# Attention in front of two expert layers: 1/sum by way of device memory, the product with v stored with a step of four, and scaling one pair later

## The chip, the cores and the metric

The kernel runs on one core of a Trainium2 chip. The metric is the time on the device in microseconds (us), the median of several executions; lower is better. The core has five engines that run side by side, each through its own instructions in order: TensorE (PE; its weight loads are shown as PEld), VectorE (DVE), ScalarE (ACT), GpSimd (POOL) and SyncE (SP), which issues all transfers (DMAs) of this kernel. TensorE writes its results into PSUM, which has eight banks per partition; the other data lies in SBUF. GpSimd doesn't work on PSUM in this kernel.

## The reference

```python
scores = np.matmul(q, k.transpose(0, 1, 3, 2)) / sqrt(64)      # 2 batches, 12 heads, 448 tokens, 64 wide
scores = np.where(causal_mask, -1e9, scores)
attn = np.exp(scores - scores.max(-1, keepdims=True))
attn = attn / (attn.sum(-1, keepdims=True) + 1e-9)
x = np.matmul(attn, v)                          # put together as 896 tokens x 768
h = x @ w_in                                    # 768 x 2048
g = np.where(h >= 1, h, np.where(h <= -1, 0, (h + 1) ** 2 / 4))
x = g @ w_out                                   # 2048 x 768
xn = x / np.sqrt(np.mean(x * x, -1, keepdims=True) + 1e-6) * rms_g
out = (silu(xn @ w_gate) * (xn @ w_val)) @ w_out2
```

q, k and v are float32; the weights are float64 and reach the chip as pairs of 32-bit words, so that each weight block has to be put together and split before TensorE can use it.

## The kernel before, in words

**The attention stage.** Heads are worked on in pairs: g runs from 0 to NG - 1 = 11 (six pairs of each batch), and j = 0, 1 are the two heads of a pair, which take partitions 0 to 63 and 64 to 127. The 448 tokens of a head are NCH = 4 chunks of C = 112. A pair has NU = 3 units u: unit 0 is the last query chunk (448 keys), unit 1 the third and the first (336 and 112 keys), unit 2 the second (224 keys). One turn of the loop at line 736 is one step n = 3 g + u, written out by hand in a fixed order for every engine. In a step, TensorE makes the scores of the next unit (line 273) and transposes the exponentials of the unit before (line 304); VectorE adds the mask and takes the maxima of this unit (line 280); ScalarE takes the exponentials with their sums (line 288); ScalarE, and for some VectorE, copy the transposed blocks of two units before out of PSUM (`evac`, lines 322 and 324). The scores rotate through four banks, the transposed blocks and the spread 1/sum through three (`tring`), and the product with v has one bank of its own (bank 7).

**1/sum.** `factor` (lines 330 and 331, VectorE) turns the sums of pair g - 1 into `rs`, 112 partitions x 2 heads x 4 chunks, in step u = 0 of pair g. In u = 1 `spread` brings these onto the layout of the result, 128 partitions x 448 tokens: 16 matmul instructions against the identity (line 338) and one copy by ScalarE into the buffer `rb` (line 340). In u = 2 `pv` multiplies by v (line 352, 20 matmul instructions). In u = 0 of pair g + 1, `xscale` (line 371, VectorE) reads the product from bank 7, multiplies by `rb` and writes the pair's place, and `xsplit` splits it into a rounded part and a rest for the layers that follow (lines 361 and 362, POOL; for pairs of the second batch subtractions by VectorE at line 358 come first). After the loop the same is written out for the last pairs, with the first matmuls of the first layer (`head_in`, `tail_in`, line 665) between them.

**Weights during attention.** The first six weight pieces (four plain blocks, two pairs of blocks) are prepared in small steps placed by hand in the table `EARLY`: (g, u) names the step of the loop, (i, j) the piece and its step. ScalarE scales (line 169), POOL makes low bits (line 180), VectorE joins the words (lines 186 and 198) and forms sums and differences (line 500), ScalarE rounds (lines 205 and 539), POOL makes the rest (lines 206 and 540). Weights arrive in three stage buffers; the last step of a piece issues the next load by SP (`w_next`, line 145). SP also issues the loads of q, k and v (lines 245, 246, 240), all in program order.

**After attention** the first layer runs as products of three operands per feature block (line 665), with weight preparation between the products; then w_out (line 968), normalisation, gate and value (line 665) and the last product (line 1280).

Of the kernel before, what the change touches and what calls it, by code (L numbers as in the profile page):

```python
# [41 lines left out]
def kernel(  # L42
# [17 lines left out]
    C = 112  # L60
# [17 lines left out]
    const = ctx.enter_context(tc.tile_pool(name="const", bufs=1))  # L78
    small = ctx.enter_context(tc.tile_pool(name="small", bufs=4))
    psum = ctx.enter_context(tc.tile_pool(name="psum", bufs=1, space=bass.MemoryType.PSUM))  # L80

# [35 lines left out]
    NPC = C * (NCH * (NCH + 1) // 2)  # L117
    NTB = 3 * NCH + 1
    Pn = AF.at(PO, 2, NPC)
# [4 lines left out]
    mask = AF.at(XFO + S, S)  # L124
    assert XFO + 2 * S <= STO
    poff = [0, C, 3 * C, 6 * C]
# [21 lines left out]

    def w_next(n):
        for i in range(n + 1, len(items)):  # L150
            if items[i][3] == items[n][3]:
                if i - n <= NST:
                    w_load(i)
                return
# [155 lines left out]
    def evac(n, i, eng):  # L310
        g, u = divmod(n, NU)
        PT = PTs[g % 2]
        t = tbank[n][i]
        if u == 2:
            out = PT[:C, :, 1:5:3, :]
            src = t[:C, :4 * C].rearrange("p (j k d) -> p j k d", j=2, k=2)
        else:
            first = 3 if u == 0 else 2
            out = PT[:C, i, first:first + 10:3, :]
            src = t[:C, :4 * C].rearrange("p (k d) -> p k d", k=4)  # L320
        if eng is nc.scalar:
            nc.scalar.copy(out, src)  # L322
        else:
            eng.tensor_copy(out, src)


    def factor(g):
# [4 lines left out]
        return rs  # L332

    def spread(rs, t=None, out=None):
        t = turn(tring) if t is None else t
        for c in range(NCH):
            for j in range(2):
                nc.tensor.matmul(t[D * j:D * (j + 1), c * C:(c + 1) * C], lhsT=rs[:C, j, c:c + 1].to_broadcast([C, D]),  # L338
                                 rhs=ident[:C, :C], start=True, stop=True, skip_group_check=True)
        nc.scalar.copy(rb if out is None else out, t[:, :S])  # L340
# [3 lines left out]
    def pv(g):  # L344
        i = g % 2
        PT = PTs[i]
        xbank[g] = xb = bank(7)
        parts = [(0, 1, C, 3 * C), (0, 11, 0, C)] + [(kc, 4 * kc, kc * C, (NCH - kc) * C) for kc in range(1, NCH)]
        for n, (kc, blk, o, w) in enumerate(parts):
            for j in range(2):  # L350
                src = PT[:C, j].rearrange("p a d -> p (a d)")[:, blk * C:blk * C + w]
                nc.tensor.matmul(xb[D * j:D * (j + 1), o:o + w], lhsT=vraw[i][:C, j, kc, :], rhs=src,  # L352
                                 start=(n == 0), stop=(n == len(parts) - 1), skip_group_check=True)
# [13 lines left out]

    def xscale(g):
        b, p = divmod(g, NP)
        x = xbank[g][:, :S] if g == NG - 1 else rb if b else X0[p]  # L370
        nc.vector.tensor_tensor(out=x, in0=xbank[g][:, :S], in1=qraw[g % NQ] if g == NG - 1 else rb, op=ALU.mult)

    def xsplit(g):
        b, p = divmod(g, NP)
        k = p % HK
        if b == 0:
            pool_split(B21 if p >= HK else B11, k, X0[p])
        elif p < HK:
            sub(rb, rb, X0[p])
            pool_split(T1, k, rb)  # L380
        else:
            t = qraw[g % NQ]
            sub(t, rb, b32(T1[:, 0, k]))
            sub(t, t, b32(T1[:, 1, k]))
            pool_split(T2, k, t)
            pool_split(B22, k, rb)

# [329 lines left out]
    def tail_in(f):  # L717
# [3 lines left out]

    EARLY = {(0, 2): ((0, 0), (0, 1), (1, 0)), (1, 2): ((0, 2),), (2, 0): ((0, 3),), (2, 2): ((1, 1),),
# [6 lines left out]

    def early(g, u):  # L730
        for i, j in EARLY.get((g, u), ()):
            pre[i][j]()

    scores(0)
    w_cap[0] = NA + 4
    for n in range(NN - 1):
        g, u = divmod(n, NU)
        scores(n + 1)
        side = nc.vector if u == 2 else nc.scalar
        old = n >= 2  # L740
# [13 lines left out]
        if u:  # L754
            exps(n, 1)
        if 0 < g and u == 2:
            pv(g - 1)
            load_v(g + 1)
        if n >= 1:
            transposes(n - 1)  # L760
        if u == 0:
            if g > 1:
                xscale(g - 2)
                xsplit(g - 2)
            if g:
                frs = factor(g - 1)
        elif u == 1 and g:
            spread(frs)
            if 1 < g < NG - 1:
                xmix(g - 2)  # L770
        early(g, u)

    n = NN - 1
    maxima(n, 0)
# [571 lines left out]
```

## Time and profile before

| | |
|---|---|
| median of 3 runs | 583.06 us (582.82 to 584.49) |
| profiled execution, its own time | 583.05 us |
| its span in the trace | 581.3 us |
| around the span | 1.75 us |
| granted TensorE clock | 1.00 of full speed throughout |
| TensorE busy | 97% of the span |
| attention stage | to about 104 us of the span |

Times of single instructions below come from the profiled execution and are counted from the start of its span. "Busy" is the time in which an engine had an instruction in work; overlapping instructions count once. The chain of waits is the work that ended last, followed back from the last instruction.

### The profile page before, as it was taken

The page shows a single profiled execution, that of the slowest core. Times are in us where ns is not written, and L with a number is a line of the kernel's source. Part 1 is how long each engine was busy: PE and PEld are TensorE (multiplying, and loading weights), DVE is VectorE, ACT ScalarE, POOL GpSimd, SP SyncE. Part 2 cuts the span into 40 slices and gives each one's busy share as a digit, 9 for nine tenths or more (in the row PEclk, how much of TensorE's full clock was granted, in tenths as well). Part 3 has the DMA queues.
Part 4 walks back from the last instruction along what each step waited for, and adds up shares of the span by engine and source line. Part 5 has one row for each costly group of instructions (what it writes and reads, how often), then busy time and mean ns, then how long its engine had stood idle before and what let it go on. Part 6 is the DMA issues. An engine that isn't in the chain of part 4 may idle for free.

```text
span 581.3 us, 8682 instructions
## 1 busy us (share of the span) xinstructions
PE 566.8 (97%) x3164; PEld 492.5 (85%) x3164; DVE 386.9 (67%) x666; ACT 350.9 (60%) x701; POOL 325.0 (56%) x256
## 2 busy tenths in 40 slices
PE   6999999989899999999999999999999999999997
PEld 3666666878789989999999998999999999999996
DVE  4877788768778877772667668776665656993110
ACT  4988988566667766665634477665545546544111
POOL 3574625845777677995645606566455455991000
PEclk9999999999999999999999999999999999999999
DMA  8334522124542336771443011345333335632002
GB/s 299 106 121 144 205 64 71 55 91 137 177 140 109 108 108 221 255 244 43 166 159 109 0 56 48 116 145 181 109 109 110 114 104 169 211 109 95 1 0 96
DMA packets 17850, 71.34 MB, mean 123 GB/s; under 512 B 2128, under 2 KB 6736, under 8 KB 17808
## 3 DMA queue, kind: packets, MB, share of 16 engines
q1 hardware_dynamic: 17808, 70.79, 36.2%
q8 instruction: 25, 0.41, 0.3%
q14 instruction: 17, 0.14, 0.1%
HBM read 68.03 MB, written 2.75 MB: 122 GB/s over the span
## 4 chain that ended last, share of the span: by engine, by line
PE 84%; DVE 6%; ACT 3%; POOL 3%; issue 2%; DMA 1%; SPq 1%; DVEq 0%; POOLq 0%; ACTq 0%
PE ps L665 34%; PE ps L968 20%; PE ps L1280 15%; PE ps L273 5%; PE ps L352 4%; PE ps L304 4%; PE ps L338 2%; POOL af L180 1%; DMA af<-in_w_in 1%; DVE af L198 1%; DVE af L358 1%; POOL ar L540 1%; DVE ps L450 1%; DVE af L450 1%; DVE af L691 0%
## 5 line engine op out<-in xcount | busy, mean ns | idle before, releaser
L665 PE MATMUL ps<-ar 128*128 128x448 f32 x1260 | 260.3, 367 | 4.9 <-ACT af L846 2.8
L665 PEld LDWEIGHTS ps<-ar 128*128 128x128 f32 x1260 | 235.1, 188 | 28.5 <-ACT af L846 4.3
L206 POOL TENSOR_TENSOR ar<-af,ar 128x768 fp32r<-128x768 f32 (+1 forms) x56 | 93.1, 1664 | 63.0 <-ACT ar L205 52.1
L968 PE MATMUL ps<-ar 128*128 128x448 f32 x576 | 118.1, 366 | 0.0
L968 PEld LDWEIGHTS ps<-ar 128*128 128x128 f32 x576 | 108.0, 188 | 9.2
L180 POOL TENSOR_SCALAR af<-af 128x768 int32<-128x768 uint8 x76 | 85.7, 1128 | 7.6 <-DMA af<-in_w_out 1.5
L1280 PE MATMUL ps<-ar 128*128 128x448 f32 x432 | 87.9, 365 | 0.0
L1280 PEld LDWEIGHTS ps<-ar 128*128 128x128 f32 x432 | 81.1, 188 | 6.7 <-DVE ar L1227 0.3
L198 DVE SCALAR_TENSOR_TENSOR af<-af 128x768 int32<-128x768 int32 (+1 forms) x66 | 72.1, 1095 | 20.3 <-POOL af L180 11.0
L169 ACT ACTIVATE af<-af 128x768 f32<-128x768 f32 x61 | 54.9, 912 | 10.5 <-DMA af<-in_w_out 10.5
L205 ACT CAST ar<-af 128x768 fp32r<-128x768 f32 (+1 forms) x56 | 41.0, 732 | 30.7 <-DVE af L198 14.7
L288 ACT ACTIVATE af<-ps,nm 112x336 f32<-112x336 f32 (+2 forms) x96 | 47.2, 507 | 9.7 <-DVE nm L280 9.6
L904 DVE TENSOR_TENSOR ar<-af,ar 128x448 fp32r<-128x448 f32 x32 | 37.8, 1191 | 21.9 <-ACT ar L903 21.9
L1227 DVE TENSOR_TENSOR ar<-af,ar 128x448 fp32r<-128x448 f32 x24 | 29.2, 1226 | 32.3 <-ACT ar L1226 32.3
L280 DVE CUSTOM_DVE_ANT_0 ps<-ps,af 112x336 f32<-112x336 f32 (+2 forms) x96 | 41.4, 472 | 8.5 <-PE ps L273 7.4
L485 POOL TENSOR_TENSOR ar<-af,ar 128x768 fp32r<-128x768 f32 x18 | 33.7, 1872 | 21.6 <-ACT ar L481 21.6
L273 PE MATMUL ps<-af 64*112 64x448 f32 (+3 forms) x192 | 37.6, 449 | 5.7 <-DVE af L251 4.4
L1061 POOL TENSOR_TENSOR ar<-af,ar 128x448 fp32r<-128x448 f32 x15 | 18.0, 1214 | 31.3 <-ACT ar L1060 15.0
L273 PEld LDWEIGHTS ps<-af 64*112 64x112 f32 x192 | 17.5, 180 | 16.4 <-DVE af L251 4.4
L304 PE MATMUL ps<-ident,af 112*112 112x112 f32 x240 | 30.4, 266 | 0.0
L304 PEld LDWEIGHTS ps<-ident,af 112*112 112x112 f32 x240 | 22.9, 133 | 6.9 <-issue 3.0
L322 ACT COPY af<-ps 112x448 f32<-112x448 f32 x47 | 24.1, 543 | 7.3 <-PE ps L304 7.0
(110 smaller groups left out, 635.9 us busy)
## 6 DMA issues: line engine op xcount, KB each, us to landing
af<-in_w_out SPq DMA_DIRECT2D x28, 768.0 KB, 4.4
af<-in_w_in SPq DMA_DIRECT2D x20, 768.0 KB, 4.4
af<-in_w_gate SPq DMA_DIRECT2D x16, 768.0 KB, 5.0
af<-in_w_val SPq DMA_DIRECT2D x12, 768.0 KB, 4.2
af<-in_kT SPq DMA_DIRECT2D x12, 224.0 KB, 4.5
af<-in_qT SPq DMA_DIRECT2D x12, 224.0 KB, 5.0
af<-in_v SPq DMA_DIRECT2D x12, 224.0 KB, 2.7
out_T<-af SPq DMA_DIRECT2D x12, 224.0 KB, 1.9
```

The lines of the kernel that those rows point to most:

```text
L169: nc.scalar.activation(c, c, ACTF.Prelu, scale=2.0 ** -112, alpha=-2.0 ** 32)
L180: nc.gpsimd.tensor_scalar(out=words(n, 0, I32), in0=b, scalar1=1.0 / 32, scalar2=-31.0 / 64, op0=ALU.mult, op1=ALU.add)
L198: nc.vector.scalar_tensor_tensor(out=out.bitcast(I32), in0=words(n, 1, I32)[:, c], scalar=3, in1=words(n, 0, I32)[:, c], op0=ALU.logical_s ...
L205: nc.scalar.copy(hi, src)
L206: nc.gpsimd.tensor_tensor(out=lo, in0=src, in1=b32(hi), op=ALU.subtract)
L273: nc.tensor.matmul(bs[j][:C, o:o + (c + 1) * C], lhsT=q[r, c * C:(c + 1) * C], rhs=k[r, :(c + 1) * C], start=True, stop=True, skip_group_c ...
L280: nc.vector.tensor_tensor_reduce(out=t, in0=t, in1=mask[:C, S - (c + 1) * C:], scale=-1.0, scalar=3e38, op0=ALU.add, op1=ALU.min, accum_ou ...
L288: nc.scalar.activation(Pn[:C, j, poff[c]:poff[c] + w], sbank[n][j][:C, o:o + w], ACTF.Exp, bias=nm[:C, j, c:c + 1], scale=-1.0, accum_out= ...
L304: nc.tensor.transpose(bs[j][:C, o:o + C], Pn[:C, j, poff[c] + kc * C:poff[c] + (kc + 1) * C], ident[:C, :C])
L665: nc.tensor.matmul(b[:, :S], lhsT=w(a, k), rhs=x[:, c, k], start=first and k == 0 and i == 0, stop=(k == HK - 1 and i == 2), skip_group_ch ...
L968: nc.tensor.matmul(ybs[dm][:, :S], lhsT=w[:, a, dm * P:(dm + 1) * P], rhs=t[:, c], start=(n == 0 and i == 0), stop=(n == NM - 1 and i == 2))
L1280: nc.tensor.matmul(obs[dm][:, :S], lhsT=w[:, a, dm * P:(dm + 1) * P], rhs=t[:, c], start=(kk == 0 and i == 0), stop=(kk == NF - 1 and i == 2))
```

## The change

- `spread` goes for ten of the twelve pairs. Instead `send` writes `rs` to device memory (a row of 2 x 448 numbers, in pieces of 4 numbers = 16 bytes, one per partition and head), in step u = 0, and `fetch` reads the row back twice, each time onto 64 partitions of `rb`, in step u = 2. Pairs 10 and 11 still use `spread`.
- So that a partition's four numbers lie side by side in that row, token c * 112 + i is now at place 4 i + c. `pv` and `spread` write their matmul results into PSUM with a step of four numbers (`chunks`); `kernel` puts the tokens back in order on the host's copy of the output.
- `pv` of pair g - 1 moves from u = 2 to u = 1 of pair g. In u = 2 ScalarE copies the product from bank 7 into SBUF (`keep`), and `xscale` multiplies there, in place, in u = 1 of the pair after; POOL does it for eight pairs, VectorE for the others.
- The loop now runs `pv` up to pair 10; the lines after the loop are as they were, so `pv(NG - 2)`, pair 10, is also run there.
- Some copies of transposed blocks go from ScalarE to VectorE or back (`MOVED`), the first of the thirteen blocks of `PT` is dropped, weight loads that a step would issue wait until u = 2 of the pair (`w_late`), and `EARLY` has other places.

```diff
-    NTB = 3 * NCH + 1
+    NTB = 3 * NCH
...
+    late = []
+    held = [True]
+
+    def w_late():
+        while late:
+            w_next(late.pop(0), True)
+
-    def w_next(n):
+    def w_next(n, now=False):
+        if held[0] and not now:
+            late.append(n)
+            return
...
+    def send(g, rs):
+        rows[g] = row = dram.tile([2, S], F32, tag="row", name="row")
+        nc.sync.dma_start(out=row.rearrange("j (p c) -> p j c", c=NCH), in_=rs[:C])
+
+    def fetch(g):
+        row = rows.pop(g)
+        for j in range(2):
+            nc.sync.dma_start(out=rb[D * j:D * (j + 1)], in_=row[j].partition_broadcast(D))
+
+    def chunks(t, j, c, n):
+        return t[D * j:D * (j + 1), :S].rearrange("p (i c) -> p c i", c=NCH)[:, c:c + n]
...
-                nc.tensor.matmul(t[D * j:D * (j + 1), c * C:(c + 1) * C], lhsT=rs[:C, j, c:c + 1].to_broadcast([C, D]),
-                                 rhs=ident[:C, :C], start=True, stop=True, skip_group_check=True)
+                nc.tensor.matmul(chunks(t, j, c, 1), lhsT=rs[:C, j, c:c + 1].to_broadcast([C, D]),
+                                 rhs=ident[:C, :C].rearrange("k (n i) -> k n i", n=1), start=True, stop=True,
+                                 skip_group_check=True)
...
-        parts = [(0, 1, C, 3 * C), (0, 11, 0, C)] + [(kc, 4 * kc, kc * C, (NCH - kc) * C) for kc in range(1, NCH)]
+        parts = [(0, 0, 1, 3), (0, 10, 0, 1)] + [(kc, 4 * kc - 1, kc, NCH - kc) for kc in range(1, NCH)]
...
-                nc.tensor.matmul(xb[D * j:D * (j + 1), o:o + w], lhsT=vraw[i][:C, j, kc, :], rhs=src,
+                nc.tensor.matmul(chunks(xb, j, o, w), lhsT=vraw[i][:C, j, kc, :], rhs=PT[:C, j, blk:blk + w],
...
-    def xscale(g):
-        b, p = divmod(g, NP)
-        x = xbank[g][:, :S] if g == NG - 1 else rb if b else X0[p]
-        nc.vector.tensor_tensor(out=x, in0=xbank[g][:, :S], in1=qraw[g % NQ] if g == NG - 1 else rb, op=ALU.mult)
+    def home(g):
+        if g < NP:
+            return X0[g]
+        if g < NG - 4:
+            return xbuf
+        return kraw[g - NG + 4] if g < NG - 2 else rb if g < NG - 1 else xbank[g][:, :S]
+
+    def keep(g):
+        nc.scalar.copy(home(g), xbank[g][:, :S])
+
+    def xscale(g, eng=nc.vector):
+        eng.tensor_tensor(out=home(g), in0=home(g) if g < NG - 2 else xbank[g][:, :S],
+                          in1=qraw[g % NQ] if g == NG - 1 else rb, op=ALU.mult)
...
-    EARLY = {(0, 2): ((0, 0), (0, 1), (1, 0)), (1, 2): ((0, 2),), (2, 0): ((0, 3),), (2, 2): ((1, 1),),
-             (3, 2): ((1, 2), (2, 0)), (4, 0): ((1, 3),), (4, 2): ((2, 1),), (5, 2): ((2, 2), (3, 0)),
-             (6, 0): ((2, 3),), (6, 2): ((3, 2), (4, 0)), (7, 0): ((3, 3),), (7, 2): ((4, 1), (4, 2)),
-             (8, 2): ((4, 3),), (9, 0): ((4, 4),), (9, 2): ((4, 5), (4, 6), (5, 0)), (10, 0): ((4, 7),),
-             (10, 2): ((4, 8),), (11, 0): ((4, 9),), (11, 1): ((4, 10),), (12, 0): ((5, 1), (5, 2)),
-             (12, 1): ((5, 3),), (12, 2): ((5, 4), (5, 5), (5, 6), (5, 7)), (12, 3): ((5, 8),),
-             (12, 4): ((5, 9), (5, 10))}
+    EARLY = {(0, 2): ((0, 0),), (1, 2): ((1, 0), (0, 1), (0, 2)), (2, 0): ((0, 3),), (2, 2): ((1, 1),),
+             (3, 2): ((1, 2),), (4, 0): ((2, 0), (1, 3)), (4, 2): ((2, 1),), (5, 2): ((2, 2), (3, 0)),
+             (6, 0): ((2, 3),), (6, 2): ((3, 2), (4, 0), (3, 3)), (7, 2): ((4, 1), (4, 2)), (9, 0): ((4, 3),),
+             (9, 2): ((5, 0),), (10, 0): ((4, 4), (4, 5)), (10, 1): ((4, 6), (4, 7), (4, 8), (4, 9)),
+             (11, 1): ((4, 10),), (12, 0): ((5, 1), (5, 2), (5, 3), (5, 4), (5, 5), (5, 6), (5, 7)),
+             (12, 3): ((5, 8),), (12, 4): ((5, 9), (5, 10))}
...
+    MOVED = [(g, 2) for g in range(NG) if g not in (3,)] + [(g, 0) for g in (0, 2, 3, 4, 6, 7)]
+    SCALED = (0, 1, 2, 3, 4, 5, 7, 8)
...
-        side = nc.vector if u == 2 else nc.scalar
+        side = nc.vector if (g, u) in MOVED else nc.scalar
...
-        if 0 < g and u == 2:
+        if u == 2 and 0 < g < NG - 1:
+            keep(g - 1)
+            fetch(g - 1)
+        if u == 2:
+            w_late()
+        if n >= 1:
+            transposes(n - 1)
+        if u == 0 and g:
+            frs = factor(g - 1)
+            if g < NG - 1:
+                send(g - 1, frs)
+        if u == 1 and g:
             pv(g - 1)
             load_v(g + 1)
-        if n >= 1:
-            transposes(n - 1)
-        if u == 0:
             if g > 1:
-                xscale(g - 2)
+                xscale(g - 2, nc.gpsimd if g - 2 in SCALED else nc.vector)
                 xsplit(g - 2)
-            if g:
-                frs = factor(g - 1)
-        elif u == 1 and g:
-            spread(frs)
-            if 1 < g < NG - 1:
-                xmix(g - 2)
+            if g == NG - 1:
+                spread(frs)
         early(g, u)
 
+    w_late()
+    held[0] = False
...
-    return np.ascontiguousarray(r.results[0]["out_T"].T)
+    out = r.results[0]["out_T"].T.reshape(B, C, S // C, DM)
+    return np.ascontiguousarray(out.transpose(0, 2, 1, 3).reshape(B * S, DM))
```

## Rows read from the trace of the kernel before

**Rows 1.** The page: span, and busy time of two engines over it.

```profile
span 581.3 us, 8682 instructions
PE 566.8 (97%) x3164; PEld 492.5 (85%) x3164; DVE 386.9 (67%) x666; ACT 350.9 (60%) x701; POOL 325.0 (56%) x256
```

**Rows 2.** Busy by window of one pair: window, length, PE, PEld, DVE, ACT, POOL, clock.

```profile
39.90:47.76 7.86, 7.86 (x74) 5.21 (x74) 5.95 (x23) 6.37 (x21) 5.24 (x5) 1.00 0.53 188
47.76:55.61 7.85, 7.85 (x74) 5.20 (x74) 5.94 (x23) 7.70 (x23) 3.15 (x5) 1.00 0.32 90
63.46:71.31 7.85, 7.85 (x74) 5.20 (x74) 6.36 (x23) 7.10 (x23) 5.20 (x5) 1.00 0.56 190
...
79.27:87.60 8.33, 8.33 (x75) 5.37 (x74) 7.19 (x26) 6.98 (x22) 3.31 (x5) 1.00 0.11 29
87.60:95.86 8.26, 8.26 (x74) 5.30 (x73) 6.14 (x21) 7.77 (x23) 2.93 (x2) 1.00 0.09 30
```

**Rows 3.** Chain of waits, one pair: start us, us, what.

```profile
47.76 0.56 PE ps L273 x4
...
49.23 0.92 PE ps L338 x16
...
51.18 2.04 PE ps L352 x20
...
55.61 0.57 PE ps L273 x4
```

**Rows 4.** Chain of waits, the start of the kernel.

```profile
12.43 1.30 DVE af L186
13.72 0.54 DVE ps L280
```

**Rows 5.** Product with v, groups by form: count, busy us, mean ns.

```profile
L352 PE MATMUL ps<-af 112*64 112x336 f32 x80 | 15.2, 459 | 0.0
...
L352 PE MATMUL ps<-af 112*64 112x112 f32 x80 | 7.2, 259 | 0.0
```

**Rows 6.** Chain of waits, the gate and value stage.

```profile
354.07 135.79 PE ps L665 x668
```

**Rows 7.** DMA issues: count, KB each, median us from issue to landing.

```profile
af<-in_v SPq DMA_DIRECT2D x12, 224.0 KB, 2.7
out_T<-af SPq DMA_DIRECT2D x12, 224.0 KB, 1.9
gvec<-in_rms_g SPq DMA_DIRECT2D x1, 3.0 KB, 5.0
```

**Rows 8.** Groups by line to 170 us: copies, products and splits of 448 columns.

```profile
L362 POOL TENSOR_TENSOR ar<-af,ar 128x448 fp32r<-128x448 f32 x15 | 18.5, 1235 | 1.3
...
L324 DVE COPY af<-ps 112x448 f32<-112x448 f32 x13 | 8.0, 616 | 0.0
...
L371 DVE TENSOR_TENSOR af<-ps,af 128x448 f32<-128x448 f32 x11 | 6.9, 624 | 10.9 <-ACT af L288 6.6 <-PE ps L352 4.3
L340 ACT COPY af<-ps 128x448 f32<-128x448 f32 x12 | 6.5, 538 | 2.0 <-PE ps L338 0.7 <-POOL ar L362 0.6
```

**Rows 9.** Waits to 170 us: engine, line, released by; us in total, times, longest.

```profile
POOL ar L361 <- DVE rs L330: 32.9, 10, 5.6
```

**Rows 10.** Timeline after attention: start, us, engine and line, idle before and releaser.

```profile
103.63 0.99 PE L338 MATMUL ps<-ident,rs 112*64 112x112 f32 x16 [0.25 <-DVE rs L331]
...
122.36 1.62 ACT L539 CAST ar<-af 128x768 fp32r<-128x768 f32 x2 [0.68 <-DVE af L500]
...
123.28 3.67 POOL L540 TENSOR_TENSOR ar<-af,ar 128x768 fp32r<-128x768 f32 x2 [9.04 <-ACT ar L539]
...
124.91 2.12 PE L665 MATMUL ps<-ar 128*128 128x448 f32 x9 [1.21 <-ACT af L840]
```

**Rows 11.** Timeline at the start: TensorE's scores around the wait.

```profile
9.98 1.65 PE L273 MATMUL ps<-af 64*112 64x448 f32 x4
...
15.14 1.24 PE L273 MATMUL ps<-af 64*112 64x224 f32 x4 [1.13 <-ACT af L288]
```

More of the change, by code (lines that the diff above doesn't have):

```diff
@@ L79 @@
     small = ctx.enter_context(tc.tile_pool(name="small", bufs=4))
+    dram = ctx.enter_context(tc.tile_pool(name="dram", bufs=2, space=bass.MemoryType.DRAM))
     psum = ctx.enter_context(tc.tile_pool(name="psum", bufs=1, space=bass.MemoryType.PSUM))
@@ L124 @@
     mask = AF.at(XFO + S, S)
-    assert XFO + 2 * S <= STO
+    xbuf = AF.at(XFO + 2 * S, S)
+    assert XFO + 3 * S <= STO
     poff = [0, C, 3 * C, 6 * C]
@@ L314, in evac @@
         if u == 2:
-            out = PT[:C, :, 1:5:3, :]
+            out = PT[:C, :, 0:4:3, :]
             src = t[:C, :4 * C].rearrange("p (j k d) -> p j k d", j=2, k=2)
         else:
-            first = 3 if u == 0 else 2
+            first = 2 if u == 0 else 1
             out = PT[:C, i, first:first + 10:3, :]
@@ L332, in factor @@
         return rs
+    rows = {}
+    def send(g, rs):
[7 more added lines that the diff above has]
+        return t[D * j:D * (j + 1), :S].rearrange("p (i c) -> p c i", c=NCH)[:, c:c + n]
     def spread(rs, t=None, out=None):
@@ L347, in pv @@
         xbank[g] = xb = bank(7)
-        parts = [(0, 1, C, 3 * C), (0, 11, 0, C)] + [(kc, 4 * kc, kc * C, (NCH - kc) * C) for kc in range(1, NCH)]
+        parts = [(0, 0, 1, 3), (0, 10, 0, 1)] + [(kc, 4 * kc - 1, kc, NCH - kc) for kc in range(1, NCH)]
         for n, (kc, blk, o, w) in enumerate(parts):
             for j in range(2):
-                src = PT[:C, j].rearrange("p a d -> p (a d)")[:, blk * C:blk * C + w]
-                nc.tensor.matmul(xb[D * j:D * (j + 1), o:o + w], lhsT=vraw[i][:C, j, kc, :], rhs=src,
+                nc.tensor.matmul(chunks(xb, j, o, w), lhsT=vraw[i][:C, j, kc, :], rhs=PT[:C, j, blk:blk + w],
                                  start=(n == 0), stop=(n == len(parts) - 1), skip_group_check=True)
@@ L375, in xsplit @@
         k = p % HK
+        x = home(g)
         if b == 0:
@@ L378, in xsplit @@
         elif p < HK:
-            sub(rb, rb, X0[p])
-            pool_split(T1, k, rb)
+            sub(x, x, X0[p])
+            pool_split(T1, k, x)
         else:
             t = qraw[g % NQ]
-            sub(t, rb, b32(T1[:, 0, k]))
+            sub(t, x, b32(T1[:, 0, k]))
             sub(t, t, b32(T1[:, 1, k]))
             pool_split(T2, k, t)
-            pool_split(B22, k, rb)
+            pool_split(B22, k, x)
     def xmix(g):
```

## The prediction, made before the changed kernel had run

> **What bounds the kernel now.** I first read the page's engine shares [rows 1]: TensorE is busy for 97% of the span, all other engines for 56% to 67%. That is an average over stages, so next came the chain of waits, which says where TensorE's time sets the end. In the attention stage the chain is TensorE alone for some 70 us: one pair is scores, transposes, spread, product with v, one behind the other, from 47.76 to 55.61, hence 7.85 us a pair, of which the spread takes 0.92 and the product 2.04 [rows 3]. Third, the busy times cut into windows of one pair [rows 2]: PE is full (7.85 of 7.85), ScalarE takes 6.37 us where a pair has no weight step, 7.10 with one and 7.70 with two, VectorE 5.95 to 6.36, POOL at most 5.24. So whatever TensorE no longer does is time won, until ScalarE at 6.4 to 7.7 us becomes the next bound; that margin is the question. Two pairs late in the stage take 8.33 and 8.26 us [rows 2], about 0.9 us over 7.85 together: there VectorE works on 1/sum, scaling, subtraction and weight sums ahead of the maxima of unit 1. Two other places are not bound by TensorE: the start, where the chain runs through VectorE's weight step at 12.43 (line 186, it waits for the first weight load), behind which its maxima start only at 13.72 [rows 4], and the weight chain right after attention, where TensorE stood idle for 1.21 us at 124.91 [rows 10].
>
> **The sum is made** against the profiled execution's 583.05 us (span 581.3 and 1.75 around it); the median of the runs is 583.06, the same for my purpose. A difference below 0.3%, 1.75 us, I take as no change.
>
> **Part 1, ten spreads less on TensorE.** Ten pairs by 0.92 us [rows 3]: -9.2 us, if nothing else becomes the bound. The pair would take 6.93 us.
>
> **Part 2, the product stored with a step of four.** No row of before shows a strided TensorE write. From below: it costs nothing. The two forms of the product differ by 224 columns and by 459 - 259 = 200 ns, so 0.89 ns a column [rows 5]; in the gate and value stage a matmul of 448 columns takes 135.79 / 668 = 0.203 us, 0.45 ns a column [rows 6]. So PSUM takes columns, side by side ones, twice as fast as the product delivers them. From above: a stored number costs twice its present time; 13 products (12, and the doubled one) by 2.04 are +26.5 us, and the two remaining spreads +1.8. I take nothing, because the product runs at half the rate that rows 6 show PSUM to take. The Trainium skill speaks against it: its page "PSUM — Partial Sum Buffer", section "Specifications (TRN2)", gives lines of 8 bytes and says that any access pattern that isn't contiguous slows matmuls significantly. By that rule the sum would land with the second rival below; no row here can confirm or refute it.
>
> **Part 3, ScalarE.** `keep` takes the place of the spread's copy, both one copy of 448 columns, 0.54 us [rows 8]: 0. Net four copies of transposed blocks go to VectorE. A pair without a weight step needs 6.37 us or less, under 6.93. One weight step adds 0.73 (7.10 - 6.37), and most such pairs lose a copy of 0.54, so they stay under 6.93. Pair 6 now holds three such steps: 6.37 + 3 x 0.73 - 0.54 = 8.0, pair 10 two: 7.8, pairs 5 and 9 one without a moved copy: 7.1. The excess over 6.93 adds up to 2.3 us. From below it is 0 where ScalarE's lead takes it up. I take the middle, +1.2. Against that stands the 0.9 us of the two long pairs of before: scaling and subtraction now come behind the maxima of unit 1, so I take that as won. Net +0.3, bounds -0.9 and +1.4.
>
> **Part 4, VectorE and POOL.** Eight scalings (0.62 us each) leave VectorE, four copies (0.62) come: -2.5 us on an engine that isn't the bound. POOL gets eight scalings; the nearest row is its own subtraction of 448 columns, 1.24 us [rows 8], and POOL waited 32.9 us in the stage for VectorE alone [rows 9], so 9.9 us fit: 0. If POOL were late, its splits would be late first, then the scaled q; the latter is made over a pair ahead.
>
> **Part 5, the way through device memory.** Issued by SP: 10 writes and 20 reads of 1/sum, 0.3 to 0.4 us each; SP has nothing else urgent. `send` goes out when `factor` is done, close to the start of u = 1. Behind it in SP's order come the loads of q and k, of v (which waits for the product, some 3.5 us into the u = 1 step), then `fetch`, which waits for the row and for `rb`, and only behind it the late weight loads. Landing: between 1.9 us (a store of 224 KB to device memory) and 5.0 (128 small pieces behind other loads) for the write, 2.7 to 5.0 for the read [rows 7]. So the row is there 2 to 5 us after the send, `fetch` goes out 4 to 5.5 us into the pair, and `rb` is full at 7 to 10.5; POOL wants it at about 7.5, one pair on (6.93 and scale_q's turn). At worst POOL waits 3 us a pair, which it has (5.24 us of work with the heaviest steps, and 1.24 of scaling, against 6.93 leave little there, more elsewhere). I take 0. The cover is POOL's idle time; without it, pair 6 and pair 9, which VectorE scales, and the subtractions from pair 6 on would hold up VectorE and with it the maxima: up to 3 us for each of five, +15 at the far end.
>
> **Part 6, the doubled product of pair 10.** It runs once in the loop and again behind it, in a stretch where TensorE before had no gap but 0.25 us [rows 10]: +2.0 (bounds 0 and 2.04). VectorE's scaling and subtractions of pair 9 come later too, into the same stretch, so TensorE might have waited there without the second product as well.
>
> **Part 7, weight steps.** At the start, the step that waits for the first weight load goes to the next pair; the maxima at 13.72 could start when their scores are done at 11.63, and TensorE's wait behind them, 1.13 us before 15.14, goes, with some 0.4 of follow-up that I estimate: -1.5 (bounds 0 and -2.1, the 13.72 - 11.63) [rows 4, 11]. After attention, the joins and sums of the sixth piece come ahead of other work, so that ScalarE does not wait 0.68 us for them before 122.36, and POOL behind it (idle until 123.28), and the chain through POOL, VectorE and TensorE moves by as much [rows 10]: -0.8 (bounds 0 and -1.2). The held loads are issued at most one pair later, to stage buffers whose data is wanted a pair or more after that: 0.
>
> **The sum:** -9.2 + 0 + 0.3 + 0 + 0 + 2.0 - 1.5 - 0.8 = -9.2, hence 573.9; I say 574.0.
>
> **Rivals.**
> - *ScalarE, or a late 1/sum, becomes the bound in most pairs.* For it: 7.10 us with one step against 6.93, and ScalarE waits in turn for VectorE and TensorE. Against: pairs without a step have 0.5 us to spare. If a pair takes 7.3 us on average in place of 6.93, ten cost 3.7 us, and the full excess of part 3 is in it: about 578, with a reach from 577 to 582. Chance 0.16.
> - *The stored step slows the product (the other side).* Place: line 352, and 338 for two pairs. At twice the time, 574 + 26.5 + 1.8 = 602 us. It turns the result to slower at a lengthening of the product by a third: 9 us over 13 x 2.04. For it: every stored number lies alone, which no row of before shows; against: rows 5 and 6. Chance 0.15. The Trainium skill's page "PSUM — Partial Sum Buffer" (section "Specifications (TRN2)") is on this rival's side; rows so far don't bear it out.
> - *1/sum arrives late and holds up VectorE.* At the far end of part 5, +15: 589; from about 2 us for each of five pairs it undoes the gain. For it: 224 pieces of 16 bytes, smaller than any in rows 7 (24 bytes). Against: some 7 us between send and use. Chance 0.05.
> - *The gain is given back after attention:* the weight chain there is bound by VectorE, ScalarE and POOL and starts from the same loads. If the stage ends 7 us earlier but the weights don't, 581.3 to 584. Against: those loads wait for buffers that the same steps set free, earlier by as much. Chance 0.04.
>
> **Chances and range.** My forecast, 571.5 to 577 by itself, has 0.60. Faster by over 0.3% (below 581.3): the forecast and nearly all of the first rival, 0.75. Within 0.3%: the last rival and the edges of others, 0.06. Slower: the strided product and the late 1/sum, 0.19. For eight in ten the range reaches from 571.5 over the first rival to 583; it leaves out the slow cases (0.19).
>
> **What would show it.** Right: one pair takes about 6.9 to 7.0 us on the chain, line 352 stays at 2.04 us for its 20 instructions and 459 ns in its long form, line 338 appears 32 times, the scores at 15.14 come at about 14, and the wait of 1.21 us after attention shrinks. Wrong: a longer line 352 (strided store); TensorE waits on line 288 or 322 in most pairs (ScalarE); long waits on line 371 or 361 for a DMA into `rb` (late 1/sum); a longer gap after 104 us less the gain (weights).

## The result, and the profile after

The changed kernel takes 575.05 us (median of 4 runs, 573.98 to 575.91), the kernel before on the same chip 583.77 us (median, 582.82 to 585.26): a ratio of 0.9847, with a 95% interval of 0.9818 to 0.9877. The profiled execution took 574.96 us, with a span of 572.9. The page of the changed kernel answers to [rows 1]:

```profile
span 572.9 us, 8453 instructions
PE 558.0 (97%) x3024; PEld 485.4 (85%) x3024; DVE 385.1 (67%) x662; ACT 347.4 (61%) x697; POOL 333.7 (58%) x264
```

TensorE is 8.8 us less busy and the span is 8.4 us shorter; the share of 97% tells nothing. One undisturbed pair on TensorE's timeline of the changed kernel (start, us, line, count; to be set beside [rows 3]):

```profile
34.47 0.64 PE L285 MATMUL ps<-af 64*112 64x224 f32 x4
35.04 0.98 PE L316 MATMUL ps<-ident,af 112*112 112x112 f32 x8
36.05 2.11 PE L378 MATMUL ps<-af 112*64 112x336 f32 x20
38.09 1.01 PE L285 MATMUL ps<-af 64*112 64x448 f32 x4
...
41.41 0.45 PE L285 MATMUL ps<-af 64*112 64x224 f32 x2
```

The spread is gone, and the product with v (now line 378) stands behind the last transposes of the pair (line 316) and ahead of the scores of 448 columns, where the spread was. From 34.47 to 41.41 that is 6.94 us; most undisturbed pairs take 6.84. The windows of one pair of the changed kernel, columns as in [rows 2] (the last two are the DMA engines' busy share and GB/s):

```profile
27.63:34.47 6.84, 6.84 (x57) 4.33 (x57) 6.35 (x22) 5.97 (x22) 5.19 (x7) 1.00 0.84 240
...
48.26:55.41 7.15, 6.92 (x57) 4.34 (x56) 6.20 (x24) 7.15 (x22) 6.04 (x6) 1.00 0.64 143
55.41:62.86 7.45, 7.45 (x56) 4.60 (x56) 5.87 (x18) 7.25 (x24) 6.95 (x7) 1.00 0.77 238
62.86:69.70 6.84, 6.84 (x57) 4.33 (x56) 6.34 (x23) 6.24 (x22) 3.20 (x4) 1.00 0.81 244
69.70:78.15 8.45, 7.13 (x57) 4.33 (x56) 6.01 (x23) 6.16 (x21) 5.04 (x6) 1.00 0.27 78
78.15:86.73 8.58, 7.65 (x56) 4.58 (x56) 8.10 (x24) 8.22 (x26) 5.81 (x5) 1.00 0.22 58
```

The reader sees four kinds of pair. Where nothing disturbs it, PE fills the window (6.84 of 6.84). In the windows from 48.26 and 55.41 ScalarE fills the first (7.15 of 7.15) and nearly the second (7.25 of 7.45). In the second PE shows as full too, 0.61 us above its 6.84: a wait between the matmuls of one group counts as busy. In the one from 69.70 no engine fills the window, so something is waited for; in the last, VectorE and ScalarE are both over 8.

The wait from 69.70 on is followed through four engines in the timeline of the changed kernel (in brackets the idle time before, and who ended it):

```profile
72.67 1.13 POOL L405 TENSOR_TENSOR af<-af 128x448 f32<-128x448 f32 x1 [1.80 <-ACT af L300]
...
73.84 0.63 DVE L384 TENSOR_TENSOR af<-af 128x448 f32<-128x448 f32 x1 [2.34 <-POOL af L405]
...
74.86 0.45 ACT L300 ACTIVATE af<-ps,nm 112x224 f32<-112x224 f32 x1 [2.29 <-DVE nm L292]
...
75.88 0.31 PE L316 MATMUL ps<-ident,af 112*112 112x112 f32 x1 [1.12 <-ACT af L334]
```

POOL scales pair 7 late (line 405); VectorE's subtraction waits for it (384), the maxima behind that hold up ScalarE's exponentials (300), and the copy behind them holds up TensorE (316). The scaling reads no result of the line that its row names as releaser; what it needs besides the kept product, written by 68.3, is 1/sum (the run with the later weight load, below, names it).

**Where the time went**, from the same points of the two profiled executions:

| stretch (start of the named work, before, after) | before | after | difference |
|---|---|---|---|
| to the scores at 24.12, 20.79 | 24.12 | 20.79 | -3.33 |
| nine pairs, to the scores at 95.86, 86.73 | 71.74 | 65.94 | -5.80 |
| to the last spread, at 103.63 [rows 10], 96.19 | 7.77 | 9.46 | +1.69 |
| to the product of the first layer at 172.86, 165.15 | 69.23 | 68.96 | -0.27 |
| to the end of the span | 408.4 | 407.7 | -0.7 |

The last line belongs to layers that the change doesn't touch. Nine pairs at 6.84 in place of 7.85 would be -9.1, and -5.80 came: the changed kernel has 3.3 us more of stalls in them than the kernel before.

### The profile page after: what moved, and what is told of

Same layout as the page of the kernel before. It is cut to its first block, busy times and chain, and to the rows that moved or that the text cites. A ratio compares the mean times of both kernels' runs of the same rounds, so it can differ in the third digit from the quotient of the medians.

```text
span 572.9 us, 8453 instructions
## 1 busy us (share of the span) xinstructions
PE 558.0 (97%) x3024; PEld 485.4 (85%) x3024; DVE 385.1 (67%) x662; ACT 347.4 (61%) x697; POOL 333.7 (58%) x264
## 4 chain that ended last, share of the span: by engine, by line
PE 71%; ACT 3%; DVE 2%; POOL 2%; issue 1%; POOLq 0%; DVEq 0%
PE ps L701 35%; PE ps L1011 20%; PE ps L1323 15%; POOL af L192 1%; ACT af L181 1%; DVE af L210 1%; DVE ps L486 0%; DVE af L486 0%; POOL af L724 0%; POOL ar L507 0%; PE ps L1096 0%; DVE ps L210 0%; DVE af L727 0%; ACT af L883 0%; ACT ar L516 0%
## 5 line engine op out<-in xcount | busy, mean ns | idle before, releaser
L192 POOL TENSOR_SCALAR af<-af 128x768 int32<-128x768 uint8 x76 | 83.9, 1104 | 7.7 <-DMA af<-in_w_out 1.5
L285 PE MATMUL ps<-af 64*112 64x448 f32 (+3 forms) x192 | 35.8, 452 | 5.0 <-DVE af L263 4.4
L1269 ACT CAST ar<-af 128x448 fp32r<-128x448 f32 x24 | 13.3, 566 | 23.7 <-PE ps L1323 23.7
```

Source lines behind the costliest of these rows:

```text
L192: nc.gpsimd.tensor_scalar(out=words(n, 0, I32), in0=b, scalar1=1.0 / 32, scalar2=-31.0 / 64, op0=ALU.mult, op1=ALU.add)
L285: nc.tensor.matmul(bs[j][:C, o:o + (c + 1) * C], lhsT=q[r, c * C:(c + 1) * C], rhs=k[r, :(c + 1) * C], start=True, stop=True, skip_group_c ...
```

## The experiments

The runs of one kernel spread over 1 to 8 us, so the worth of a single place is read from these points of the profiled executions, and the medians say whether the whole moved.

### Does a step of four cost anything?

**The product stored side by side** (1/sum keeps the order of its row, so numbers meet the factor of another token, and the output has other values):

```diff
-        return t[...].rearrange("p (i c) -> p c i", c=NCH)[:, c:c + n]
+        return t[...].rearrange("p (c i) -> p c i", c=NCH)[:, c:c + n]
```

> The changed kernel with one edit: the product with v and the two remaining spreads are stored side by side again instead of with a step of four (1/sum stays in the order of the row, so numbers meet the factor of another token). Theory (the step is free, because this product writes a column only every 0.89 ns): within 1 us of the changed kernel, 574 to 576 us, line 378 with 458 ns in its long form as now. Rival (the step costs something that the other savings hide): faster than the changed kernel by 2 us or more, and the long form below 450 ns.

Measured: 577.35 us (573.52 to 578.78), ratio 0.9866 [0.983, 0.9901]; last spread at 96.18, as in the changed kernel (96.19). The median lies 1.4 us above the range that was expected; the six runs spread over 5 us, and at the last spread the two kernels stand equal. By form, with the step (changed kernel) and then side by side (count, busy us, mean ns):

```profile
L378 PE MATMUL ps<-af 112*64 112x336 f32 x104 | 19.7, 458 | 0.0
...
L378 PE MATMUL ps<-af 112*64 112x112 f32 x104 | 9.4, 259 | 0.0
```

```profile
L378 PE MATMUL ps<-af 112*64 112x336 f32 x104 | 19.7, 458 | 0.1
```

The mean is that of [rows 5] to a nanosecond, with the step and without. So the step is free here. That doesn't say why, which the next two runs ask.

**The same step where columns come twice as fast.** In both runs the matmuls of line 701 (the first layer, and gate and value) use only the upper halves of weights and activations, as bf16; the second also stores them with the step, so the layers see reordered columns (lines shortened):

```diff
-    nc.tensor.matmul(b[:, :S], lhsT=w(a, k), rhs=x[:, c, k], ...
+    nc.tensor.matmul(b[:, :S], lhsT=w(a, k).bitcast(BF16)..., rhs=x[:, c, k].bitcast(BF16)..., ...   # first run
+    nc.tensor.matmul(b[:, :S].rearrange("p (i c) -> p c i", c=NCH), ...            # second run
```

> The changed kernel, in which the matmuls of the first layer (448 columns each, line 701) take only the upper 16 bits of weights and activations, as bf16, and store side by side: the partner for the next run. Its values are then coarser; the number of instructions stays. Both theories: a matmul of 448 columns there takes 0.19 to 0.21 us, as in the gate and value stage of the kernel before (0.203 us).

> As the run before, but each matmul of the first layer stores its 448 columns with a step of four, as the product with v does. Theory A (a step is free only because the product delivers a column per 0.89 ns, half of what PSUM takes): here, at about 0.45 ns a column, each matmul gets longer, towards 0.4 us, and the stage nearly doubles. Theory B (a step of four costs nothing at any rate): the same mean time as in the run before within 2%.

Measured, one run each: 568.89 us and 783.9 us. By form, side by side and then with the step:

```profile
L701 PE MATMUL ps<-ar 128*128 128x448 bf16 x1260 | 252.0, 358 | 6.4 <-ACT af L891 2.7 <-DVE af L729 1.8 <-POOL ar L507 0.6
```

```profile
L701 PE MATMUL ps<-ar 128*128 128x448 bf16 x1260 | 474.6, 577 | 0.0
```

Matmuls overlap, so the busy time over the count is the rate: 252.0 / 1260 = 0.200 us for 448 columns, 0.45 ns a column; with the step 474.6 / 1260 = 0.377 us, 0.84 ns a column. The 222.6 us more account for the 215.2 us by which the span grew (566.8 to 782.0). So theory B is out and theory A's forecast came: a stepped store of bf16 matmuls goes in at about 0.84 ns a column. The fp32 product delivers one per (458 - 259) / 224 = 0.89 ns by its mean times, whose ends are modelled; by its starts in the changed kernel (336 columns at 23.08, the next 336 at 23.36, the next matmul at 23.64) it is 0.28 us for 336, 0.83 ns a column. So the product is no faster than the step allows, but there is no margin either that these runs could show. That the rate is the reason, and not the type of the operands, is argued: the two runs change the rate by the type. The Trainium skill's page "PSUM — Partial Sum Buffer", section "Specifications (TRN2)", holds that any access pattern that isn't contiguous slows matmuls significantly. The bf16 run agrees with it (0.45 to 0.84 ns a column), the product with v doesn't (459 and 458 ns).

### What opened the pair?

The prediction credited the pair's gain to the ten spreads alone. Four runs separate them from the other thing that moved on TensorE, the product (from the step of unit 2 to that of unit 1).

**Kernel before, ten spreads' matmuls left out** (ScalarE's copy kept, on 112 partitions; 1/sum does not reach those ten pairs):

```diff
-        for c in range(NCH):
+        for c in range(NCH if mm else 0):
...
-        nc.scalar.copy(rb if out is None else out, t[:, :S])
+        nc.scalar.copy((rb if out is None else out)[r], t[r, :S])
...
-            spread(frs)
+            spread(frs, mm=g == NG - 1)
```

> The kernel before with one edit: the matmuls of ten of the twelve spreads are left out, the copy by ScalarE stays (1/sum does not reach those ten pairs). Theory (the stage is bound by TensorE and ten spreads are worth 0.92 us each): 583.5 - 9.2 = about 574 us, with pairs of 6.9 us on TensorE. Rival (without the other rearrangements ScalarE and VectorE become the bound at once): 577 us or more, with waits of TensorE on lines 288 and 322.

Measured: 585.11 us (581.84 to 589.5, 12 runs), ratio 1.0017 [0.9991, 1.0042]: nothing gained. In seven of the twelve the mean granted clock of TensorE is 0.993 or 0.994; in the profiled one it is 0.50, the lower of the two levels, from 20 to 24 us of the span, behind 4 us (14 to 18) in which TensorE was busy for 2.3. The other five, at 0.999 or 1.000, have a median of 582.59 us, 0.8 below the kernel before on the same chip (583.39), where 9.2 were expected. The chain of waits, one pair at full clock (start, us, what):

```profile
36.65 1.80 PE ps L273 x4
38.45 2.04 PE ps L353 x20
40.49 0.91 PE ps L304 x8
41.40 0.95 PE ps L273 x8
42.35 0.53 PE ps L304 x4
...
44.49 1.82 PE ps L273 x4
46.30 2.04 PE ps L353 x20
```

A pair is still 7.85 us, from 38.45 to 46.30. The scores of 448 columns now take 1.8 us where they had 1.04: they absorb what the spread gave up. The timeline of the same run says for what they wait (PEld is TensorE's weight load):

```profile
42.91 0.53 ACT L322 COPY af<-ps 112x448 f32<-112x448 f32 x1
43.42 0.54 ACT L288 ACTIVATE af<-ps,nm 112x336 f32<-112x336 f32 x1
...
45.04 0.21 ACT L288 ACTIVATION_READ_ACCUMULATOR af<-ps,nm 112x1 f32 x1
...
45.30 0.27 PEld L273 LDWEIGHTS ps<-af 64*112 64x112 f32 x2 [0.57 <-ACT af L288]
```

That is a closed loop over two engines. On TensorE: product 2.04, transposes 0.91, scores 0.95, transposes 0.53 (to 42.88); then on ScalarE the copy of those transposes from 42.91 and, behind it in its order, the exponentials up to 45.25 (45.04 + 0.21); these free the bank in which the second half of the next scores goes (45.30), and behind them stands the next product (46.30). The trace of the kernel before has the same loop:

```profile
26.35 0.21 ACT L288 ACTIVATION_READ_ACCUMULATOR af<-ps,nm 112x1 f32 x1
26.51 0.37 PEld L273 LDWEIGHTS ps<-af 64*112 64x112 f32 x4
26.52 1.10 PE L273 MATMUL ps<-af 64*112 64x448 f32 x4
```

The four loads take 0.37 us, not 0.27 as in the changed kernel (at 24.31): those of the second half begin at 26.61, 0.05 us behind the end of the exponentials (26.56), as in the run without spreads (45.30 and 45.25), and the scores take 1.03 us up to the product at 27.55, where the changed kernel takes 0.94 (38.09 to 39.03 above). So the loop was the longer one even then, by some 0.1 us against TensorE's own sum of 7.76 (the changed kernel's 6.84 and the spread's 0.92). The chain showed no wait, because it lay between the matmuls of one group.

**Changed kernel, product put back to the step of unit 2:**

```diff
         if u == 2 and 0 < g < NG - 1:
+            pv(g - 1)
+            load_v(g + 1)
             keep(g - 1)
...
         if u == 1 and g:
-            pv(g - 1)
-            load_v(g + 1)
```

> The changed kernel with one part undone: the product with v (and the load of the next v) goes back from u = 1 to u = 2, ahead of the copy that empties its bank; 1/sum still goes through device memory. Theory (before, a loop took 7.85 us a pair beside TensorE's own sum: product, transposes, scores and transposes on TensorE, then a copy and the exponentials of unit 1 on ScalarE, which the next scores wait for; the earlier place of the product is what breaks it): pairs of 7.7 to 8.0 us and 581 to 585 us, although ten spreads are gone. Rival (the spreads alone are the gain, as the prediction has it): pairs of 6.85 us and about 573 us, the second product of pair 10 being gone too.

Measured: 587.9 us (586.28 to 591.07), ratio 1.009 [1.0066, 1.0114], with pairs of 7.85 us (products at 25.59 and 33.45) and longer, so above the 581 to 585 that were expected. The clock is not the reason: the one run with a mean of 1.000 took 586.73. With every other part of the change in place, and ten spreads gone, the whole gain is gone.

**Kernel before, product early, spreads kept** (and the second product not made):

```diff
-        if 0 < g and u == 2:
+        if n >= 1:
+            transposes(n - 1)
+        if 0 < g and u == 1:
             pv(g - 1)
             load_v(g + 1)
-        if n >= 1:
-            transposes(n - 1)
...
-    pv(NG - 2)
```

> The kernel before with one part of the change: the product of pair g - 1 (and the load of the next v) moves from u = 2 to u = 1, ahead of the spread, and pair 10's product behind the loop is left out since the loop now makes it. All spreads stay. Theory: TensorE's own sum stays 7.85 us a pair, so 582 to 584 us, no change. Rival (the place of the product is the whole gain): 576 us or less.

Measured: 588.86 us (588.03 to 589.35), ratio 1.0098 [1.0085, 1.0112]: slower, which neither theory had. TensorE's timeline of this run, behind product and spread:

```profile
36.53 1.01 PE L273 MATMUL ps<-af 64*112 64x448 f32 x4
38.15 0.98 PE L304 MATMUL ps<-ident,af 112*112 112x112 f32 x8 [0.61 <-ACT af L322]
```

The spread now comes behind the product, ScalarE's copy of it later still, and the copy of the transposed blocks, in order behind that one, holds up the transposes: pairs of 8.29 us (33.72 to 42.00).

**Both edits on the kernel before** (no row sent through device memory, no work moved between engines; 1/sum does not reach ten pairs): the two diffs on the kernel before together.

> The kernel before with both: the product in u = 1 and the matmuls of ten spreads left out, their copies kept (1/sum does not reach those pairs); no transfers, no work moved between engines. Theory (both together, neither alone, open the pair): 6.9 to 7.1 us a pair, 573 to 577 us. Rival (copies and scalings on other engines have to move as well): 579 us or more, with waits of TensorE on ScalarE in most pairs.

Measured: 576.24 us (575.65 to 577.11), ratio 0.9885 [0.9871, 0.9898], pairs of 6.84 to 7.6 us. So, as ratios to the kernel before: spreads out 1.0017, product early 1.0098, both 0.9885: each alone gains nothing, and together they open the pair.

### The smaller terms

**The second product of pair 10 left out** (nothing else of the computation changes):

```diff
     xmix(NG - 3)
-    pv(NG - 2)
```

> The changed kernel with one edit: the second product of pair 10, behind the loop, is left out. Theory of the prediction (TensorE has no gap there): faster by up to 2.0 us, about 573. Rival (VectorE's scaling and subtractions, which also moved there, are the next wait): within 0.7 us of the changed kernel, with a new wait of TensorE for line 342 or 343.

Measured: 573.62 us (572.13 to 577.64), ratio 0.9826 [0.9794, 0.9857]. From one remaining spread to the other it takes 4.22 us (89.76 to 93.98) in place of 5.94 (90.25 to 96.19): the second product costs 1.7 us.

**The first weight steps as before the change:**

```diff
-    EARLY = {(0, 2): ((0, 0),), (1, 2): ((1, 0), (0, 1), (0, 2)), ...
+    EARLY = {(0, 2): ((0, 0), (0, 1), (1, 0)), (1, 2): ((0, 2),), ...
```

> The changed kernel with one edit: the weight steps of the first two pieces at the start are placed as before, so VectorE's sign step comes ahead of the maxima of pair 1. Theory: slower by 1.5 to 2.3 us than the changed kernel, with the scores now at 13.95 us at about 15.1. Rival (the margin at the start is used up by another wait): within 0.7 us.

Measured: 577.14 us (575.76 to 579.69), ratio 0.9881 [0.9853, 0.9908]. The first scores after the wait come at 15.79 (changed 13.95), those one pair on at 23.25 (changed 20.79), and the 2.5 us stay to the last spread (98.69 and 96.19). Part of it is a later landing: POOL, for which VectorE's step waits, begins on the first weight load at 12.18 in this run, in the kernel before at 11.49:

```profile
12.18 0.87 POOL L179 TENSOR_SCALAR af<-af 128x768 f32<-128x768 f32 x1 [2.58 <-DMA af<-in_w_in]
```

```profile
11.49 0.90 POOL L167 TENSOR_SCALAR af<-af 128x768 f32<-128x768 f32 x1 [2.54 <-DMA af<-in_w_in]
```

So by this run the start is worth between 1.8 and 2.5 us. The kernel before against the changed one gives 2.3: the 3.33 us of the table less the 1.01 that this pair gains like every other.

**The weight load held in pair 7, issued one pair later:**

```diff
-        if u == 2:
+        if u == 2 and g != 7:
             w_late()
```

> The changed kernel with one edit: the weight load held in pair 7 is issued in pair 8 instead. In the changed kernel pair 9 takes 8.4 us, VectorE waits 2.34 us for POOL's scaling, which starts late after the reads of 1/sum. Theory (that weight load, 768 KB, delays q and 1/sum on the way): VectorE's wait goes below 1 us, pair 9 below 7.6, and 0.8 to 1.5 us are won, some of which pair 10 may give back. Rival (the scaling is late for another reason): same wait, within 0.7 us.

Measured: 575.67 us (573.82 to 576.23), ratio 0.9868 [0.9852, 0.9885]; last spread at 94.37, pair 9 takes 7.16 us (69.66 to 76.81) and VectorE's wait in it 1.04. POOL's scaling of pair 7, first in the run with the plain store, whose order of instructions here is the changed kernel's, then in this one:

```profile
72.62 1.14 POOL L405 TENSOR_TENSOR af<-af 128x448 f32<-128x448 f32 x1 [1.84 <-DMA af<-row]
```

```profile
71.30 1.14 POOL L405 TENSOR_TENSOR af<-af 128x448 f32<-128x448 f32 x1 [1.14 <-DMA af<-row]
```

Both rows name the read of 1/sum: the scaling starts when that has landed. SP's rows show one reason why it is late: it issues the two reads, which wait until the row is written, from 66.94 with the load later, right behind the load of v (66.44), but from 67.89 in the changed kernel and 68.81 in the run with the plain store. How much the load does is less plain: in six executions whose order of instructions is the same up to there, the two pairs around it (from 62.86 to 78.15 in the changed kernel) take 14.4 us twice and 14.8 to 15.4 four times, with the load later 14.0 and 14.1 (the second is the last run below). So 1/sum comes late by chance of the landing too, and moving the load takes between 0.3 and 1.3 us off these two pairs; the median doesn't show it.

**The sixth weight piece's steps as before the change:**

```diff
-             (11, 1): ((4, 10),), (12, 0): ((5, 1), (5, 2), (5, 3), (5, 4), (5, 5), (5, 6), (5, 7)),
-             (12, 3): ((5, 8),), (12, 4): ((5, 9), (5, 10))}
+             (11, 1): ((4, 10),), (12, 0): ((5, 1), (5, 2)), (12, 1): ((5, 3),),
+             (12, 2): ((5, 4), (5, 5), (5, 6), (5, 7)), (12, 3): ((5, 8),), (12, 4): ((5, 9), (5, 10))}
```

> The changed kernel with the steps of the sixth weight piece after attention back where they stood before the change (two in the first place, one in the second, four in the third). Theory A (the prediction's part 7): the new places gain 0.8 us, so this run is 0.8 us slower than the changed kernel, span about 573.7. Theory B (bringing them forward puts VectorE's sums ahead of the clips that TensorE waits for, and loses what it gains): span 572.2 to 572.9, and the wait of TensorE on the clip, 1.64 us in the changed kernel, falls back towards 1.2 us or less.

Measured: 576.68 us (574.16 to 579.01), ratio 0.9881 [0.9854, 0.9907], which doesn't tell it from the changed kernel. TensorE after attention, changed kernel and then this one:

```profile
96.19 0.99 PE L364 MATMUL ps<-ident,rs 112*64 112x112 f32 x16
...
115.46 4.83 PE L701 MATMUL ps<-ar 128*128 128x448 f32 x21 [1.64 <-DVE af L727]
...
165.15 15.06 PE L701 MATMUL ps<-ar 128*128 128x448 f32 x73 [0.36 <-POOL ar L507]
```

```profile
94.88 0.99 PE L364 MATMUL ps<-ident,rs 112*64 112x112 f32 x16
...
116.14 2.10 PE L701 MATMUL ps<-ar 128*128 128x448 f32 x9 [1.18 <-ACT af L883]
...
164.14 16.08 PE L701 MATMUL ps<-ar 128*128 128x448 f32 x78 [0.39 <-POOL ar L507]
```

New places: 68.96 us from the spread to the product behind line 507; old ones 69.26 here and 69.23 before. The new places are worth 0.3 us by one execution each, theory A's 0.8 did not come. As theory B had it, the wait on ScalarE (1.18) is gone, but the joins and sums on VectorE now stand ahead of the clip of line 727, and TensorE waits 1.64 us for that. That this run's spread is 1.3 us early is pairs 9 and 10 again, whose instructions are the same in both; so neither theory's span can be read here.

**The single product and the later load together:**

> The changed kernel with the two edits that won time each by itself: the second product of the last pair but one left out, and the weight load of pair 7 issued in pair 8. Theory A (the two lie in different pairs and add up): the second of the remaining spreads comes at 96.2 - 2.2 - 1.8 = 92.2 us, span 568.9, median about 571. Theory B (the stretch behind attention is bound by the weight chain, which the later load holds up): the spread comes at 92.2 but the span stays at 570 to 572.

Measured: 572.53 us (572.08 to 575.51, 5 runs), ratio 0.9818 [0.9794, 0.9841], the lowest median of the kernels that compute all of it in full; its interval overlaps the changed kernel's. The last spread comes at 92.87, span 570.2. The two don't add up to the end (92.2 and 568.9 by theory A): part of the second was chance, and 0.6 us more lie in the later layers, which no edit touches. Theory B's span came (570 to 572), but its hold-up isn't there, for from the spread to the product behind line 507 it is 68.93 us, as in the changed kernel.

## Why the prediction was right, and where it wasn't

The forecast of 574.0 was 1.0 us from the median. Its terms, against what the traces gave:

| term | predicted | measured |
|---|---|---|
| part 1, ten pairs | -9.2 | -10.1 |
| part 2, step of four | 0 | 0 |
| parts 3 to 5, stalls (net of the two long pairs) | +0.3 | +3.3 |
| part 6, second product | +2.0 | +1.7 |
| part 7, start | -1.5 | -2.3 |
| part 7, after attention | -0.8 | -0.3 |
| later layers, and around the span | 0 | -0.4 |
| sum | -9.2 | -8.1 |

The measured ten pairs are ten of 1.01, one of them out of the 3.33 us of the table above, whose rest is the start; +3.3 is 9.1 less 5.80. The last line but one is -0.7 and the 0.3 us more that lie around the span (1.75 and 2.06); the profiled executions differ by 8.1.

- **Part 1: right size, wrong reason.** The step that failed is "so whatever TensorE no longer does is time won". The run without spreads won nothing (1.0017). A second loop, over TensorE and ScalarE, took 7.85 us a pair, some 0.1 more than TensorE's own sum. The product's move, which the prediction did not price at all, takes 2.04 us out of it; the 0.1 is why a pair gained 1.01 and not 0.92. That the size came right is luck: the edit that breaks the loop was part of the same change. A chain of waits that lies on one engine doesn't show a loop of nearly the same length beside it. In [rows 2] PE was busy for 7.85 of 7.85 and ScalarE for as little as 6.37, and I read the difference as a margin, without adding up the path that goes through both.
- **Part 2: right, by a margin that isn't there.** I took nothing because PSUM takes columns side by side twice as fast as the product delivers. The runs show a stepped store at 0.84 ns a column against the product's 0.83 to 0.89: the second rival failed at the edge, not by a factor of two.
- **Part 3: mis-sized.** The places were right, three steps in pair 6 and two in pair 10, but I took the middle of an excess of 2.3 us, and it came in full and more. The pair from 48.26 takes 0.31 and the next 0.61 us too long, with ScalarE full; pair 10 takes 8.58 (predicted 7.8; 8.1 in the executions in which pair 9 is short), where VectorE, which I had taken to be relieved, is busy for 8.10. The 0.9 us of the two long pairs was not won: the same two are long again.
- **Part 4: right in its cost.** POOL's eight scalings take 9.9 us, 1244 ns each, as costed. But where POOL was late, in pair 9, it was VectorE's subtraction that waited first, not POOL's own splits.
- **Part 5: right but for pair 9.** Write and reads of 1/sum, in the changed kernel's DMA issues (count, KB each, median us to landing):

```profile
af<-row SPq DMA_DIRECT2D x20, 112.0 KB, 3.1
row<-rs SPq DMA_DIRECT2D x10, 3.5 KB, 3.9
```

  Both medians lie in the ranges given (single landings of the reads and writes go from 1.5 to 6.0 us). In pair 9 the third rival came true for one pair: the cover, POOL's idle time, was not enough, POOL waited, and VectorE with it, as part 5 had named for the subtractions, for 1.6 us of that pair at most (8.45 - 6.84).
- **Part 7:** the start, 2.3, lies just past its bound of 2.1. The bound ended at the first maxima: to the scores at 15.14 and 13.95 it is 1.2 us, and the pair behind them, 8.98 us before in place of 7.85, gave another 1.1. After attention the wait of 1.21 us [rows 10] did not shrink but became one of 1.64 us for another engine.
- **Rivals:** the first (ScalarE in most pairs) came true in pairs 6 and 7 only, and with VectorE in pair 10; the fourth did not occur, 0.27 us more was won after the stage.

So the sum was near by luck, because errors met: stalls 3.0 us and the stretch after attention 0.5 us worse than said; pairs 0.9, start 0.8, the second product 0.3 and the untouched stretches 0.4 us better.

## What to carry to other kernels

Before crediting removed work with its whole time, add up the loops that pass through the same engine and one other: here TensorE was full, yet taking 0.92 us a pair from it gave nothing until the product left the path from transposes to the freed bank. The wait of such a loop can hide in a group of matmuls that takes a little longer than the same group elsewhere (here 1.03 us for 0.94). An edit that is free at one rate need not be so at another: measure it at the faster rate too before using it elsewhere. Where a value goes through device memory with a pair of slack, look for the one pair in which a bulk load is issued ahead of it.

## What the runs showed of the hardware that was not expected

- fp32 matmuls of 336 columns into PSUM took 458 ns with a step of four words and side by side (0.83 to 0.89 ns a column); bf16 matmuls with the same step went from 0.45 to 0.84 ns a column.
- A write of 1/sum to device memory in pieces of 16 bytes (3.5 KB in all) landed in 3.9 us at the median, about as fast as a load of 224 KB of v beside it (3.8 us).
- With ten spreads out of the kernel before, the granted clock fell to 0.50 for some microseconds early in the attention stage in the profiled run, and seven of its twelve runs show a mean of 0.993 or 0.994.
- With the same order of instructions, the use of a value read from device memory began at 71.8 us in some executions and at 72.7 in others, and the pairs behind it differed by 1.3 us; that is part of the scatter of the medians.
